# Last item divided on chip by products with constant selections, and the last block's output projection, layer norm and first MLP steps tile by tile

## The chip, the cores and the metric

The kernel runs on one core of a Trainium2 chip. The metric is the device time of one execution in microseconds (us); the median of three runs stands for a kernel. A profiled execution is a further run of its own, with its own time.

## The reference

One transformer layer on 2048 rows of 512 numbers, 32 heads of width 16, a hidden width of 1792, all float32:

```python
x = A_x
h = x + _A_ref(_layernorm(x, axis=-1), A_wqkv, A_wo)     # softmax attention, then @ wo
h2 = h + _B_ref(_layernorm(h, axis=-1), B_w1, B_w2)      # silu(z @ w1) @ w2
return h2
```

## The kernel before

**Precision.** A float32 product is made of three products of rounded operands (type float32r): high x high, low x high, high x low. `product` (L101) yields these three matmuls for each chunk of 128 contraction rows, 512 columns each. "Split" below means a copy to the rounded high part and a subtraction for the low part (`low`, L89).

**Attention.** The work goes in 32 items (`ITEMS`): an item is four heads for one block of 512 query rows, eight items to a block. In an item, 16 steps (`c`) each make four score products (`scores`, L463), four exponentials on ACT and, two steps later, four products with the values (`values`, L474), which accumulate in the one PSUM bank `pv`; row 16 of each head's 32 rows is the softmax denominator. `finish_item` (L489) copies `pv` to `pvs` and sends it on by DMA: denominators to DRAM and back as 16 per row (`sums`), a reciprocal on DVE (`invert`), to DRAM again and back broadcast over each head's 16 rows (`spread`, tile `den`), and, for each pair of items, one multiplication (`divide`) of a quarter of `ot`. `ot` holds attention's output of a block, transposed, in four chunks of 128 features for four tiles (`t`) of 128 rows; items 30 and 31 fill the lower and the upper 64 partitions of the last chunk.

**After a block**: output projection with `wo` (`project_rows`, L564), addition of the input rows and statistics (`add_rows`, L572), normalization (`normalize`, L158, on DVE), transposition on TensorE with a split into `hth` and `htl` (`turn`, L161), then the MLP (`mlp`, L581): 14 hidden chunks `f`, each with 12 matmuls for the first product, SiLU on ACT, a split, and 12 matmuls (three for each of the four tiles) for the second product, one chunk later. For the first three blocks this lies among the next block's attention. The last block has nothing beside it: `finish_last` (L649) runs it after the last value product.

**Order.** Every engine's instructions are pinned to the order in which the code issues them, and `soon(n, fn)` places a function n steps later. So an instruction that waits holds up all that stand behind it on its engine. Bank pools: `st` has four PSUM banks, `sm` three, `pv` one. Weight halves rotate through two buffers per name, raw weights through four.

Of the kernel before, what the change touches and what calls it, by code (L numbers as in the profile page):

```python
# [9 lines left out]
F32 = mybir.dt.float32  # L10
# [4 lines left out]
ALU = mybir.AluOpType  # L15
# [44 lines left out]
def attention_mlp_kernel(ctx: ExitStack, tc: tile.TileContext, x, wqkv, wo, w1, w2, out):  # L60
# [100 lines left out]
    def turn(src, dst_h, dst_l):  # L161

        ps = bank("ps_tr").rearrange("p (c n) -> p c n", n=P)
# [298 lines left out]

    def scores(g, k):  # L463
# [25 lines left out]
    def finish_item(i):  # L489
# [3 lines left out]
        act("copy", pvs, pv)  # L493
        dma(dn[i], pvs.rearrange("(k r) n -> k r n", r=32)[:, DH, :])
# [7 lines left out]
    rcs = {}  # L502
# [18 lines left out]
    def divide(i):  # L521

        o = ot[i // 8 % 2][:, :, i % 8 // 2, :]
        if i < ITEMS - 1:
            pool("tensor_tensor", o, o, den[i // 2], ALU.mult)
        else:
            dve("tensor_tensor", o, o, den[i // 2], ALU.mult)
# [15 lines left out]
    def split_weights(kind, f, engine):  # L543
        if f < FC:
            w = raw_w.pop((kind, f))
            wh, wl = ws[kind, f] = [gp.tile([P, 512], F32R, name=kind + part) for part in "hl"]
            act("copy", wh, w)
# [30 lines left out]
    def turn_rows(t):  # L578
        turn(hx.pop(t), hth[:, :, t * P:(t + 1) * P], htl[:, :, t * P:(t + 1) * P])

    def mlp(b, beside):  # L581
        engine = "pool" if beside else "dve"
# [3 lines left out]

        def second(f, gh, gl):
            w2h, w2l = ws.pop(("w2", f))
            if f == 0:
                acc.append(bank("ps_acc"))  # L590
            for t in range(4):
                weave(product(acc[t], lambda c: gh[:, t * P:(t + 1) * P], lambda c: gl[:, t * P:(t + 1) * P],
                              lambda c: w2h, lambda c: w2l, 1, start=f == 0, stop=f == FC - 1),
                      beside if f < FC - 1 else None)
                if f == FC - 1:
                    n = 4 * b + t
                    h = rows_of(b, t)
                    dve("tensor_tensor", h, acc[t], h, ALU.add)
                    dma(out[n * P:(n + 1) * P, :], h)

        last = None
        for f in range(FC):
            tick()
            if f < 2:
# [4 lines left out]
            split_weights("w1", f + 1, engine)  # L609
            split_weights("w2", f, engine)  # L610
# [3 lines left out]
            g, gh, gl = (bp.tile([P, 512], dt, tag="pt", name=name)  # L614
                         for name, dt in (("g", F32), ("gh", F32R), ("gl", F32R)))
            act("activation", g, ps, AF.Silu)
            act("copy", gh, g)
            low(gl, g, gh)
            if last:
                second(*last)  # L620
            last = (f, gh, gl)
        if b < NB - 1:

            act("activation", small.tile([P, 1], F32, name="sw"), ident[:, :1], AF.Exp)
        second(*last)
# [22 lines left out]

    def finish_last(pending):  # L649

        b, i = NB - 1, ITEMS - 1
        O = ot[b % 2]
# [12 lines left out]
        for t in range(4):  # L665
            run(project_rows(t, ps[t], range(3), stop=False))
        divide(i)
        for t in range(4):
            act("copy", os[t][0][:, 3:], O[:, t, 3:])
            low(os[t][1][:, 3:], O[:, t, 3:], os[t][0][:, 3:])  # L670
        act("activation", small.tile([P, 1], F32, name="sw"), ident[:, :1], AF.Silu)
        found = {}
        for t in range(4):
            run(project_rows(t, ps[t], [3], start=False))
            found[t] = add_rows(b, t, ps[t])
            if t > 0:
                normalize(hx[t - 1], rows_of(b, t - 1), *found[t - 1])
        normalize(hx[3], rows_of(b, 3), *found[3])
        for t in range(4):
            turn_rows(t)  # L680
        mlp(b, None)
# [19 lines left out]
    for g in range(groups):  # L701
# [20 lines left out]
        if g == groups - 4:  # L722
            for t in range(4):
                load_rows(NB - 1, t)
            for w in first_weights.values():
                load_weights(*w)
# [44 lines left out]
```

## Time and profile before

| | us |
|---|---|
| median of 3 runs (lowest, highest) | 1742.24 (1742.16, 1743.16) |
| profiled execution, its time | 1743.91 |
| span of that execution | 1742.1 |
| end of the last exponential | 1633.4 |
| last matmul begins | 1737.7 |

Times in the profile count from the start of the span. A row of a timeline has the start, the duration, engine, line and operation, then out<-in, shape and count; in brackets stand the idle time before it and what ended that. PE are matmuls, PEld the loads of the stationary operand, DVE, ACT and POOL the other engines, SP issues the DMAs. All matmuls of products have line 67, vector operations line 84, activations and copies line 81, POOL operations line 74, transpositions line 70: one helper records each kind, so groups are told apart by their tiles.

### The profile page before, as it was taken

The page shows a single profiled execution, that of the slowest core. Times are in us where ns is not written, and L with a number is a line of the kernel's source. Part 1 is how long each engine was busy: PE and PEld are TensorE (multiplying, and loading weights), DVE is VectorE, ACT ScalarE, POOL GpSimd, SP SyncE. Part 2 cuts the span into 40 slices and gives each one's busy share as a digit, 9 for nine tenths or more (in the row PEclk, how much of TensorE's full clock was granted, in tenths as well). Part 3 has the DMA queues.
Part 4 walks back from the last instruction along what each step waited for, and adds up shares of the span by engine and source line. Part 5 has one row for each costly group of instructions (what it writes and reads, how often), then busy time and mean ns, then how long its engine had stood idle before and what let it go on. Part 6 is the DMA issues. An engine that isn't in the chain of part 4 may idle for free.

```text
span 1742.1 us, 28292 instructions
## 1 busy us (share of the span) xinstructions
PE 1690.5 (97%) x10466; PEld 655.0 (38%) x10466; DVE 1461.3 (84%) x2392; ACT 1262.3 (72%) x2507; POOL 229.2 (13%) x312
## 2 busy tenths in 40 slices
PE   7999999999999999999999999999999999999899
PEld 5666322222245532222245532222245532221377
DVE  6899899999978889999978889999978889994243
ACT  4223699999953269999953269999963279999643
POOL 2123200000033300000033300000033300000000
PEclk9999999999999999999999999999999999999999
DMA  5334301111212111111213111111222111100232
GB/s 184 100 92 151 110 30 32 36 50 34 63 56 88 55 48 31 35 50 36 62 57 88 56 47 31 35 45 41 62 68 77 55 48 32 36 8 11 64 91 73
DMA packets 102211, 103.11 MB, mean 59 GB/s; under 512 B 20344, under 2 KB 78776, under 8 KB 102072
## 3 DMA queue, kind: packets, MB, share of 16 engines
q1 hardware_dynamic: 102072, 101.30, 19.9%
q8 instruction: 82, 1.34, 0.3%
q14 instruction: 57, 0.47, 0.1%
HBM read 77.86 MB, written 17.30 MB: 55 GB/s over the span
## 4 chain that ended last, share of the span: by engine, by line
PE 51%; ACT 36%; DVE 10%; issue 1%; DMA 1%; SPq 1%; POOL 0%; ACTq 0%; POOLq 0%; DVEq 0%
ACT pt L81 35%; PE pv L67 19%; PE ps_s L67 8%; PE ps_m L67 7%; DVE mx L206 6%; PE ps_qk L67 5%; PE ps_acc L67 5%; PE ps_v L67 3%; PE ps_wo L67 2%; DVE gl L84 2%; PE ps_tr L70 1%; DVE ot L84 1%; PE ps_w L67 1%; ACT pvs L81 1%; DMA w<-in_B_w_dram 0%
## 5 line engine op out<-in xcount | busy, mean ns | idle before, releaser
L206 DVE TENSOR_REDUCE mx<-ps_m 128x1 f32<-128x512 f32 x2048 | 1283.4, 684 | 124.3 <-PE ps_m L67 97.2
L81 ACT ACTIVATE pt<-ps_s 128x512 f32<-128x512 f32 x2048 | 1018.7, 645 | 33.8 <-PE ps_m L67 33.3
L67 PE MATMUL ps_s<-qs,ks 64*128 64x512 f16 x2048 | 550.8, 381 | 9.6 <-ACT pt L81 1.8
L67 PE MATMUL pv<-pt,va 128*17 128x512 f32 x4096 | 540.8, 601 | 1.0
L67 PE MATMUL ps_m<-ks,qs 48*128 48x512 f16 x2048 | 528.5, 382 | 8.9 <-DVE mx L206 7.1
L67 PEld LDWEIGHTS <-ks 64*128 64x128 f16 x2048 | 152.8, 95 | 538.3 <-issue 433.5
L67 PEld LDWEIGHTS pv<-pt,va 128*17 128x17 f32 x4096 | 68.8, 95 | 242.3 <-issue 226.1
L67 PEld LDWEIGHTS <-qs 48*128 48x128 f16 x2048 | 123.5, 94 | 84.2 <-issue 76.6
L81 ACT ACTIVATE g<-pv 128x512 f32<-128x512 f32 x52 | 31.1, 597 | 146.3 <-PE pv L67 146.3
L74 POOL TENSOR_SCALAR nm<-nm 128x16 f32<-128x16 f32 x32 | 8.3, 259 | 681.9 <-DVE nm L213 662.0
L84 DVE TENSOR_TENSOR gl<-g,gh 128x512 fp32r<-128x512 f32 x56 | 58.8, 1049 | 44.3 <-ACT gh L81 44.3
L67 PE MATMUL ps_acc<-w2h,gh 128*128 128x512 f32 x224 | 92.1, 411 | 0.0
L67 PE MATMUL ps_acc<-w2l,gh 128*128 128x512 f32 x224 | 91.5, 409 | 0.0
L81 ACT CAST w2h<-w 128x512 fp32r<-128x512 f32 x56 | 34.8, 621 | 73.7 <-POOL w1l L74 41.0
L67 PE MATMUL ps_acc<-w2h,gl 128*128 128x512 f32 x224 | 88.2, 394 | 0.0
L67 PE MATMUL pv<-hth,w1l 128*128 128x512 f32 x208 | 87.4, 420 | 0.0
L67 PE MATMUL pv<-htl,w1h 128*128 128x512 f32 x208 | 83.8, 403 | 0.0
L67 PE MATMUL pv<-hth,w1h 128*128 128x512 f32 x208 | 83.8, 403 | 0.0
L74 POOL TENSOR_TENSOR w1l<-w,w1h 128x512 fp32r<-128x512 f32 x42 | 54.2, 1291 | 153.4 <-ACT w1h L81 139.6
L74 POOL TENSOR_TENSOR w2l<-w,w2h 128x512 fp32r<-128x512 f32 x42 | 53.7, 1278 | 57.3 <-ACT w2h L81 57.3
L81 ACT ACTIVATE ks<-ps_qk,qk_s 128x512 f32<-128x512 f32 x24 | 16.5, 687 | 56.9 <-PE ps_qk L67 56.9
L74 POOL TENSOR_TENSOR ot<-ot,den 128x512 f32<-128x512 f32 x15 | 19.1, 1275 | 268.8 <-DMA den<-dr 255.4
(100 smaller groups left out, 1209.2 us busy)
## 6 DMA issues: line engine op xcount, KB each, us to landing
w<-in_B_w_dram SPq DMA_DIRECT2D x112, 256.0 KB
ks<-kd SPq DMA_DIRECT2D x120, 192.0 KB
qs<-qd SPq DMA_DIRECT2D x128, 48.0 KB
kd<-sh SPq DMA_DIRECT2D x16, 256.0 KB
qd<-sh SPq DMA_DIRECT2D x16, 256.0 KB
ot<-pvs SPq DMA_DIRECT2D x128, 32.0 KB
den<-dr SPq DMA_DIRECT2D x128, 32.0 KB
hx<-in_A_x_dram SPq DMA_DIRECT2D x16, 256.0 KB
```

The costliest lines, as they stand in the source:

```text
L67: tc.keep_in_program_order(nc.tensor.matmul(*a, **k))
L70: tc.keep_in_program_order(nc.tensor.transpose(*a))
L74: tc.keep_in_program_order(getattr(nc.gpsimd, op)(*a, **k))
L81: pin(getattr(nc.scalar, fn)(*a, **k))
L84: pin(getattr(nc.vector, fn)(*a, **k))
L206: pin(nc.vector.tensor_reduce(mx[i][:, j, a, qt, kb:kb + 1], ps, axis=AX.X, op=ALU.max))
```

## The change

1. **The last item (31)** isn't sent through DRAM. Two constant 128x128 selections, made on POOL before the attention loop, multiply `pvs` on TensorE in plain float32: `ps_d` gets each head's denominator on that head's 16 rows, `ps_o` the head's output. DVE takes the reciprocal of 64x512 and multiplies. Item 30 is divided by itself on 64 partitions.
2. **Splits of the last block** move into item 31, on DVE: the first three chunks of `ot`, item 30's half of the fourth, and the first two chunks of `w1` (high part too). They go into `hth` and `htl`, which are free then. The loads of rows and weights come some steps earlier.
3. **Tile by tile**: each tile is projected, added, normalized (tiles 0 to 2 on POOL, tile 3 on DVE) and transposed for itself, and `begin(t)` makes the first product of hidden chunks 0 and 1 for that tile alone: 24 matmuls of 128 columns.
4. **MLP of the last block**: written out as a loop, with the second product two chunks behind the first; the first products of chunk 2 onwards go to `sm` banks.

```diff
+    for k, (a, j) in enumerate(HEADS):
+        rows = slice(64 + 16 * (2 * a + j), 80 + 16 * (2 * a + j))
+        pool("tensor_copy", sel_o[:, rows], ident[:, 32 * k:32 * k + 16])
+        pool("tensor_copy", sel_d[:, rows], ident[:, 32 * k + DH:32 * k + DH + 1].to_broadcast([P, 16]))
...
     def finish_last(pending):
...
-        for t in range(4):
-            os[t] = [bp.tile([P, DC, P], F32R, tag="pt", name=name) for name in ("oh", "ol")]
-            act("copy", os[t][0][:, :3], O[:, t, :3])
-            low(os[t][1][:, :3], O[:, t, :3], os[t][0][:, :3])
         for g in pending:
             values(g)
-        agenda.clear()
-        sums(i)
-        invert(i)
-        spread(i)
-        split_weights("w1", 0, "dve")
-        ps = [bank("ps_wo") for _ in range(4)]
-        for t in range(4):
-            run(project_rows(t, ps[t], range(3), stop=False))
-        divide(i)
...
+        pvs = last.pop()
         act("activation", small.tile([P, 1], F32, name="sw"), ident[:, :1], AF.Silu)
+        ps_o, ps_d = bank("ps_o"), bank("ps_d")
+        ps_rows = [bank("ps_wo", "sm") for _ in range(3)] + [bank("ps_wo")]
+        first = [project_rows(t, ps_rows[t], range(3), stop=False) for t in range(4)]
+        for _ in range(3):
+            next(first[0])
+        mm(ps_d, sel_d, pvs, start=True, stop=True)
+        mm(ps_o, sel_o, pvs, start=True, stop=True)
+        o = bp.tile([P, 512], F32, tag="pt", name="o")
+        dve("reciprocal", o[64:], ps_d[64:])
+        dve("tensor_tensor", o[64:], ps_o[64:], o[64:], ALU.mult)
+        act("copy", hth[64:, DC - 1, :], o[64:])
+        low(htl[64:, DC - 1, :], o[64:], hth[64:, DC - 1, :])
...
+        run(first[0], first[1])
+        begun = [bank("ps_w1") for _ in range(2)]
+        def begin(t):
+            cols = slice(t * P, (t + 1) * P)
+            for f in range(2):
+                w1h, w1l = (w.rearrange("p (c n) -> p c n", n=P) for w in ws["w1", f])
+                run(product(begun[f][:, cols], lambda c: w1h[:, c, :], lambda c: w1l[:, c, :],
+                            lambda c: hth[:, c, cols], lambda c: htl[:, c, cols], DC))
...
+        rest(0)
+        rest(1)
+        run(first[2])
+        rest(2)
+        add(0)
+        norm(0)
+        add(1)
+        norm(1)
+        turn_first(0)
+        run(first[3])
+        rest(3)
+        add(2)
+        norm(2)
+        turn_first(1)
+        turn_second(0)
+        begin(0)
+        add(3)
+        norm(3)
+        turn_second(1)
+        turn_first(2)
+        begin(1)
+        turn_first(3)
+        turn_second(2)
+        begin(2)
+        turn_second(3)
+        begin(3)
...
-        if g == groups - 4:
-            for t in range(4):
-                load_rows(NB - 1, t)
-            for w in first_weights.values():
-                load_weights(*w)
+        if i == ITEMS - 1:
+            if c < 4:
+                load_rows(NB - 1, c)
+                split_early(c)
+            if c == 4:
+                for f in range(3):
+                    load_weights("w1", f)
+                for f in range(2):
+                    soon(5, split_weights, "w1", f, "dve", "dve")
```

`rest(t)` is the fourth chunk's three matmuls of the projection, `add` and `norm` are the addition with statistics and the normalization, `turn_first` the four transpositions and the high copy on ACT, `turn_second` the low part on DVE.

DVE, from the last maximum's reduction (`nm<-mx`, the row ahead of these) through the projection, before:

```order
L84 RECIPROCAL rc<-rc 128x16
L84 TENSOR_TENSOR ol<-ot_2033,oh 128x384 x4
L84 RECIPROCAL rc<-rc 128x16
L84 TENSOR_TENSOR w1l<-w,w1h 128x512
L84 TENSOR_TENSOR ot_2033<-ot_2033,den 128x4x128
L84 TENSOR_TENSOR ol<-ot_2033,oh 128x128 x4
L84 TENSOR_TENSOR ot_2033<-ps_wo,hx 128x512
L84 BN_STATS st<-ot_2033 128x6
L84 BN_AGGR mv<-st 128x2
```

and in the change, from item 30's reciprocal on:

```order
L84 RECIPROCAL rc<-rc 128x16
L84 CAST w1h<-w 128x512
L84 TENSOR_TENSOR w1l<-w,w1h 128x512
L84 CAST w1h<-w 128x512
L84 TENSOR_TENSOR w1l<-w,w1h 128x512
L84 CAST hth<-ot_2033 64x512
L84 TENSOR_TENSOR htl<-ot_2033,hth 64x512
L84 RECIPROCAL o<-ps_d 64x512
L84 TENSOR_TENSOR o<-ps_o,o 64x512
L84 TENSOR_TENSOR htl<-o,hth 64x512
L84 TENSOR_TENSOR ot_2033<-ps_wo,hx 128x512
L84 BN_STATS st<-ot_2033 128x6
```

The reciprocal of 128x16 behind a DMA has become one of 64x512 behind a matmul, and the splits now stand ahead of it.

ACT, from the last copy of `pv` to the weights of the MLP's first chunks, before:

```order
L81 COPY pvs<-pv 128x512
L81 CAST w1h<-w 128x512
L81 CAST oh<-ot_2033 128x128 x4
L81 ACT_TABLE_LOAD
L81 ACTIVATE sw<-ident 128x1
L81 CAST hth<-ps_tr 128x4x128 x4
L81 CAST w1h<-w 128x512
L81 CAST w2h<-w 128x512
L81 ACTIVATE g<-ps_w_21406 128x512
L81 CAST gh<-g 128x512
```

and in the change:

```order
L81 COPY pvs<-pv 128x512
L81 ACT_TABLE_LOAD
L81 ACTIVATE sw<-ident 128x1
L81 CAST hth<-o 64x512
L81 CAST hth<-ps_tr 128x4x128 x4
L81 ACTIVATE g<-ps_w_21310 128x512
L81 CAST gh<-g 128x512
L81 CAST w1h<-w 128x512
L81 ACTIVATE g<-ps_w_21311 128x512
L81 CAST gh<-g 128x512
```

The next high part of `w1` (chunk 2) now stands behind the SiLU and its copy, where before chunk 1's stood ahead of them.

More of the change, by code (lines that the diff above doesn't have):

```diff
@@ L613, in mlp, with gate, second @@
                           lambda c: hth[:, c, :], lambda c: htl[:, c, :], DC), beside)
[L614 to L618, printed above, removed]
-            if last:
[L620 to L625, printed above, removed]
+            gs = gate(ps)
+            if last:
+                second(b, *last, acc, beside)
+            last = (f, *gs)
+        act("activation", small.tile([P, 1], F32, name="sw"), ident[:, :1], AF.Exp)
+        second(b, *last, acc, beside)
+    def gate(ps):
+        g, gh, gl = (bp.tile([P, 512], dt, tag="pt", name=name)
+                     for name, dt in (("g", F32), ("gh", F32R), ("gl", F32R)))
+        act("activation", g, ps, AF.Silu)
+        act("copy", gh, g)
+        low(gl, g, gh)
+        return gh, gl
+    def second(b, f, gh, gl, acc, beside):
+        w2h, w2l = ws.pop(("w2", f))
+        while f == 0 and len(acc) < 4:
+            acc.append(bank("ps_acc"))
+        for t in range(4):
+            weave(product(acc[t], lambda c: gh[:, t * P:(t + 1) * P], lambda c: gl[:, t * P:(t + 1) * P],
+                          lambda c: w2h, lambda c: w2l, 1, start=f == 0, stop=f == FC - 1),
+                  beside if f < FC - 1 else None)
+            if f == FC - 1:
+                n = 4 * b + t
+                h = rows_of(b, t)
+                dve("tensor_tensor", h, acc[t], h, ALU.add)
+                dma(out[n * P:(n + 1) * P, :], h)
     found = {}
@@ new lines, in add, with norm, turn_first @@
+        def add(t):
+            h = rows_of(b, t)
+            dve("tensor_tensor", h, ps_rows[t], hx[t], ALU.add)
+            found[t] = statistics(h)
+        def norm(t):
+            if t < 3:
+                mv, rs = found[t]
+                pool("tensor_scalar", hx[t], rows_of(b, t), mv[:, 0:1], rs, op0=ALU.subtract, op1=ALU.mult)
+            else:
+                normalize(hx[t], rows_of(b, t), *found[t])
+        parts = {}
+        def turn_first(t):
+            ps = bank("ps_tr", "sm").rearrange("p (c n) -> p c n", n=P)
+            for c in range(4):
+                tr(ps[:, c, :], hx[t][:, c * P:(c + 1) * P], ident)
+            h = hth[:, :, t * P:(t + 1) * P]
+            act("copy", h, ps)
+            parts[t] = ps, h
```

103 lines of the change are left out of this document (62 added, 41 removed).

## The prediction, as put on record before the run

> **What bounds the kernel now.** The page first: engine shares and the slices of the span.
>
> ```profile
> PE 1690.5 (97%) x10466; PEld 655.0 (38%) x10466; DVE 1461.3 (84%) x2392; ACT 1262.3 (72%) x2507; POOL 229.2 (13%) x312
> PE   7999999999999999999999999999999999999899
> ```
>
> PE is busy for 97%; of the 40 slices only the first and the third last are below nine tenths. TensorE's order in the two kernels is the same up to the last value product, but for names of buffers, so the question is the stretch behind it. Next the table of stretches, cut where PE's work changes (columns: stretch, length, then busy time and count of PE, PEld, DVE, ACT, POOL, clock, DMA):
>
> ```profile
> 1605.90:1634.50 28.60, 27.45 (x181) 5.04 (x181) 0.95 (x3) 28.60 (x61) 0.00 (x0) 1.00 0.27 75
> 1634.50:1643.00 8.50, 8.50 (x40) 6.65 (x36) 2.06 (x5) 1.48 (x4) 0.00 (x0) 1.00 0.10 18
> 1643.00:1646.70 3.70, 0.15 (x2) 0.01 (x1) 0.72 (x2) 0.36 (x2) 0.00 (x0) 1.00 0.55 157
> 1646.70:1651.40 4.70, 4.60 (x12) 3.04 (x12) 4.34 (x12) 2.03 (x5) 1.16 (x3) 0.64 0.04 16
> 1651.40:1658.50 7.10, 3.57 (x17) 2.30 (x17) 6.18 (x13) 2.42 (x5) 2.58 (x6) 0.74 0.01 2
> 1658.50:1663.00 4.50, 4.50 (x13) 3.54 (x14) 1.84 (x3) 0.96 (x2) 0.00 (x0) 0.65 0.35 117
> 1663.00:1736.10 73.10, 73.10 (x316) 59.17 (x315) 25.81 (x39) 31.36 (x53) 0.00 (x0) 1.00 0.26 76
> ```
>
> Item 31 is ACT's (28.60 of 28.60), with DVE and POOL free. Then come 36 matmuls of the projection (8.5 us), a hole of 3.7, the projection's last 12 at a clock of 0.64, a chain of normalizations and transpositions with PE half idle, a first MLP product at 0.65, and from 1663.0 to the end PE without a gap. The chain of waits says what fills hole and chain:
>
> ```profile
> 1638.73 1.75 DMA rc<-dn
> 1640.78 1.40 DMA dr<-rc
> 1643.48 1.81 DMA den<-dr
> 1645.61 0.70 DVE ot L84
> ...
> 1656.08 0.56 DVE hx L84
> ...
> 1658.47 4.49 PE ps_w L67 x12
> 1662.96 2.80 PE pv L67 x12
> 1665.76 2.76 PE ps_acc L67 x12
> 1668.52 2.81 PE pv L67 x12
> ```
>
> The DMA round trip ends in the division at 1645.61; DVE's chain holds the first product back to 1658.47. A product at full clock takes 2.81 (0.234 a matmul), a second one 2.76. Everything behind is PE's, and has the same matmuls in both kernels. So I compare one point: where chunk 0's second product begins with products 0, 1 and 2 done. Before, products 0 to 2 and chunk 0's second product are done at 1668.52 + 2.81 = 1671.33, so the point stands at 1671.33 - 2.76 = 1668.57.
>
> **The division.** ACT's four splits no longer stand ahead of the copy of `pv`; the last value product sets its start:
>
> ```profile
> 1631.77 2.77 PE L67 MATMUL pv<-pt,va 128*17 128x512 f32 x24
> L67 PE MATMUL pv<-pt,va x4096: 592/593/1061, 201.0 to 1633.9; 128*17 128x512 f32 x196
> L81 ACT COPY pvs<-pv 128x512 f32<-128x512 f32 x32 | 20.1, 629 | 2.1 <-PE ps_n L70 1.6 <-PE pv L67 0.5
> L84 DVE RECIPROCAL qk_e<-qk_s x1: 164/164/164, 26.7 to 26.7; 128x1 f32<-128x1 f32 x1
> L84 DVE RECIPROCAL rc<-rc 128x16 f32<-128x16 f32 x32 | 7.8, 244 | 25.9 <-DMA rc<-dn 25.9
> L84 DVE TENSOR_TENSOR ot<-ot,den 128x512 f32<-128x512 f32 x1 | 0.7, 691 | 4.3 <-DMA den<-dr 4.3
> ```
>
> The values end at 1631.77 + 2.77 = 1634.54, the copy (0.63) at 1635.2. The 24 records are six sets of four side by side, two for each float32 product, so a set takes (2.77 - 0.59)/5 = 0.435 and a plain float32 product of 512 columns 0.87. `ps_d` starts at 1635.25 and lands at 1636.3 (0.435 + 0.593). The reciprocal's price is unseen at 512 columns. From 1 to 16 columns it grew by 244 - 164 = 80 ns, 5.33 ns a column; so 0.16 + 511 x 0.00533 = 2.9. Its bounds are 0.69, the multiplication at one pass, and 7.8 (244 ns for every 16). I take 2.9: same operation, two sizes. It ends at 1639.2, the multiplication at 1639.9, ACT's copy (0.62) at 1640.55, the low part (0.69) at 1641.25.
>
> PE meanwhile does the two selections and 15 projection matmuls: 1635.25 + 1.74 + 15 x 0.234 = 1640.5. The fourth chunk's second matmul needs the low part: a stall of 0.6 to 0.8. So the 3.7 us hole shrinks to that, paid with 1.74 of new PE work.
>
> The Trainium skill, "VectorE: DVE Perf Modes", section "First, the fixed hardware budget", says that the reciprocal divides iteratively with a repeat count of 8. If that meant eight cycles at its 0.96 GHz, the estimate were 512 x 8 / 0.96 = 4.3 us and the sum 1.4 later; the two rows give 5.1 such cycles a column, and I go by them.
>
> **The chain of tiles.** Rows for its steps, tile 1's normalization then POOL's nearest:
>
> ```profile
> 1650.03 0.69 DVE L84 BATCH_NORM_STATS2 st<-ot 128x6 f32<-128x512 f32 x1
> 1651.03 0.42 POOL L74 TENSOR_SCALAR rs<-mv 128x1 f32<-128x1 f32 x1 [0.64 <-DVE mv L84]
> 1651.54 0.56 POOL L74 TENSOR_TENSOR rs<-rs,expo 128x1 f32<-128x1 f32 x1
> L74 POOL TENSOR_TENSOR ot<-ot,den 128x512 f32<-128x512 f32 x15 | 19.1, 1275 | 268.8 <-DMA den<-dr 255.4 <-DMA ks<-kd 13.3
> 1651.43 0.66 PE L70 MATMUL ps_tr<-ident,hx 128*128 128x128 f32 x4
> L70 PE MATMUL ps_tr<-ident,hx x64: 272/273/476, 496.6 to 1657.4; 128*128 128x128 f32 x64
> ```
>
> From 1641.3 two matmuls of `rest(0)`, `rest(1)`, nine of `first[2]` and `rest(2)` keep PE for 17 x 0.234, to 1645.25. DVE's addition and statistics are 0.69 + 0.69 + some 0.2 for the aggregate = 1.6, from the landing of `rest(0)` at 1641.9 to 1643.55; POOL's root adds 1.05. POOL's normalization of 128x512 is unseen: bounds 0.56 (DVE's own, in the chain above) and 1.28 (POOL's two-input form); I take 1.2, near POOL's row. So tile 0 is ready at 1645.85: a stall of 0.6. The next tiles come from POOL every 2.2 and are ready before PE asks. Four transpositions are 0.45 of PE's time, the twelve matmuls of `first[3]` and `rest(3)` 2.8, four more transpositions 0.45: `begin(0)` starts at 1649.6.
>
> **The narrow matmuls** decide: 96 of 128 columns in place of 24 of 512 (24 x 0.234 = 5.6 us). No row has a float32r matmul below 512 columns. Nearest:
>
> ```profile
> 1634.47 0.19 PEld L67 LDWEIGHTS ps_wo<-wo_h,oh 128*128 128x128 f32 x1 [0.85 <-ACT oh L81]
> 1634.47 0.51 PE L67 MATMUL ps_wo<-wo_h,oh 128*128 128x512 f32 x1
> 1634.58 0.19 PEld L67 LDWEIGHTS ps_wo<-wo_h,ol 128*128 128x128 f32 x1
> 1635.05 0.40 PE L67 MATMUL ps_wo<-wo_l,oh 128*128 128x512 f32 x1
> ```
>
> The first load is followed 0.11 later by the second, and its matmul is 0.11 longer (0.51 against 0.40): a load occupies the array for 0.11, however wide the matmul. Four 128-column transpositions in 0.66 with 0.273 for one give 0.11 to 0.13 each as well. So the price per matmul lies between 0.06 (a quarter of 0.234) and 0.234 (no gain from narrowness); I take 0.115, load-bound.
>
> Then 96 x 0.115 + two sets of transpositions (0.9) end `begin(3)` at 1661.6. The DVE and ACT parts are ready in time: tile 3's addition (from 1649.3), root and normalization end at 1652.6 and tile 1's low part, queued behind them on DVE, at 1653.3, when `begin(1)` has just started. Behind `begin(3)` comes a new wait. Chunk 2's weights need the buffers of chunk 0, read until 12 matmuls before the end (1660.2, landing 1660.4), and stand behind SiLU and copy. How long that series takes, the steady MLP shows:
>
> ```profile
> 1715.96 0.60 ACT L81 ACTIVATE g<-pv 128x512 f32<-128x512 f32 x1 [2.42 <-PE pv L67]
> 1717.12 0.62 ACT L81 CAST w1h<-w 128x512 fp32r<-128x512 f32 x1
> 1717.86 0.68 DVE L84 TENSOR_TENSOR w1l<-w,w1h 128x512 fp32r<-128x512 f32 x1
> ```
>
> That is 2.58 us: the low part of `w1` is there at 1663.0, a stall of about 1.2 in PE. Eleven matmuls of chunk 2 are left (2.57): the point is reached at **1665.57, 3.0 us earlier** than before's 1668.57. Later chunks have the old rhythm, with the second product two chunks behind, so their splits have more room, not less. With the price x of a narrow matmul the point moves by 84x - 12.65 us (96 in the path, 12 taken off since the weights' wait starts 12 earlier): zero at x = 0.15.
>
> The page "TensorE: Matmul & The Clock Gate" of the Trainium skill, section "Back-to-back issue gap", has 81 ns for sustained 128-column pairs. Worked out as an estimate that would put the sum at -5.8; no run here shows it for float32r, and the load of 0.11 speaks against it.
>
> **At nothing** I cost: item 31's new splits (12 DVE operations of at most 0.7; DVE is busy 0.95 of 28.6; were it not free, each would cost that), the earlier loads on SP, the SiLU table (under the selections; ACT waits until 1639.9), the banks (each one taken anew has its reader done by then), and POOL's ten small operations before the loop, where it idles 20.15 us:
>
> ```profile
> 214.37 1.28 POOL L74 TENSOR_TENSOR wo_l<-w,wo_h 128x512 fp32r<-128x512 f32 x1 [20.15 <-PE ps_s L67]
> ```
>
> Sum: 1743.91 - 3.0 = 1740.9 for a run like the profiled one, which lies 1.7 above the median; the same 3.0 off 1742.24 gives **1739.2**. That is -0.17%, and about 0.2% (3.5 us) is what a measurement of this kernel can tell from no change.
>
> **The rivals.** *R1, slower: narrow float32r at the plain float32 rate.* 0.87 per 512 columns is 0.217 per 128. Place: the four `begin`s; price 84 x 0.217 - 12.65 = +5.6, so 1747.9; it decides from 0.15 on. For it: the operands are float32 in the rows. Against: at 512 columns float32r takes a quarter of float32's time. Chance 0.15.
>
> *R2: load and matmul don't overlap* at this width: 0.11 + 0.053 = 0.16, or PEld's whole 0.188. +0.8 to +3.1, so 1743.0 to 1745.3. Against: transpositions overlap. Chance 0.13.
>
> *R3: the clock.* Two rows of stretches:
>
> ```profile
> 1644.40:1647.80 3.40, 1.11 (x4) 0.86 (x5) 1.60 (x6) 1.44 (x5) 0.00 (x0) 1.00 0.52 164
> 1647.80:1651.30 3.50, 3.50 (x9) 2.19 (x7) 3.36 (x8) 0.94 (x2) 1.06 (x3) 0.52 0.00 0
> ```
>
> 3.4 us with PE a third busy are followed by as long at half clock. Load-bound narrow matmuls keep the array half used, and the stall of 1.2 stands right behind them; one such stretch costs 1.7, leaving -1.3, 1740.9. A reciprocal of 4.3 would end near there too. Chance 0.10.
>
> **How the numbers follow.** Forecast 0.57: x from 0.107 to 0.13 and POOL's bounds give -4.6 to -1.5, 1737.6 to 1740.7. R1 0.15, R2 0.13, R3 0.10, and 0.05 for a stall I don't see, counted as slower. The range, 1737.4 to 1745.6, holds the forecast, R3 and R2, 0.80. Faster by over 0.2% (under 1738.8) is nearly half of the forecast, 0.27; slower (over 1745.7) R1 and the 0.05, 0.20; within, 0.53.
>
> **What will show it.** Right: no DMA between the last value product and the projection's end; a 64x512 reciprocal of 2.9; narrow matmuls 0.11 to 0.12 apart; an ACT wait ahead of chunk 2's product; the clock at 1.00 throughout. Wrong: narrow starts over 0.15 apart, a reciprocal over 4, POOL's normalization over 1.5, or a clock of 0.5 within the `begin`s.

## The result and the profile after

The changed kernel takes **1741.08 us** (median of 20 runs, 1736.14 to 1748.58), the kernel before 1741.31 (20 runs beside them, 1736.69 to 1744.06); the ratio is 1.0005, 95% interval [0.9993, 1.0016]. No difference can be told. The forecast gain of 3.0 us would be a ratio of 0.9983, which lies outside this interval: the time came out within the range, which contains the old time as well, but the gain did not come.

The profiled execution took 1741.04 us with a span of 1739.3, against 1743.91 and 1742.1 before. But most of these 2.8 us lie ahead of the change. The last block's first projection matmul starts at 1634.47 before and at 1632.15 after, 2.3 us earlier, and the attention ahead of it is the same work. At the last exponential of item 24, at 1294.6 us before, the traces are 0.8 us apart, at that of item 25 they are 2.3 apart. One stretch between the two shows why; its row in the table of stretches of the kernel before (columns: stretch, length, busy time and count of PE, PEld, DVE, ACT, POOL, clock, DMA):

```profile
1412.30:1415.70 3.40, 3.39 (x15) 0.59 (x15) 1.56 (x4) 2.43 (x6) 0.67 (x3) 0.52 0.02 5
```

and the same stretch in the changed kernel:

```profile
1412.30:1415.70 3.40, 3.37 (x28) 0.94 (x23) 2.65 (x5) 3.40 (x10) 0.42 (x2) 1.00 0.00 0
```

Before, TensorE ran at half clock there and did 15 matmuls in place of 28; that comes and goes between executions (7 of the 14 traces have half clock there). So spans of two executions can't be compared for an edit at the end. I compare **the tail**: from the first projection matmul to the end of the span.

| | before | after | forecast |
|---|---|---|---|
| tail, us | 107.6 | 107.15 | 104.6 |
| first projection matmul to chunk 0's second product, with products 0 to 2 done | 34.10 | 33.85 | 31.1 |
| granted clock up to that point | 0.5 and 1.0 by turns | 1.00 | 1.00 |

The tail is 0.5 us shorter, not 3.0, though its clock stayed at 1.00. The page's share of PE is what it was:

```profile
PE 1692.2 (97%) x10542; PEld 659.6 (38%) x10542; DVE 1465.4 (84%) x2394; ACT 1257.8 (72%) x2498; POOL 237.4 (14%) x326
```

The chain that ended last, changed kernel (start, length, engine and tile):

```profile
1634.09 3.37 DVE o L84
...
1638.93 0.70 DVE htl L84
...
1639.68 0.74 PE ps_wo L67 x2
...
1643.15 2.08 POOL hx L74
...
1646.18 2.08 POOL hx L74
...
1649.22 2.08 POOL hx L74
...
1652.19 0.55 DVE hx L84
1652.74 0.61 DVE htl L84
...
1653.39 2.68 PE ps_w L67 x22
...
1662.42 0.70 DVE w1l L84
...
1663.16 2.83 PE ps_w L67 x11
1666.00 2.76 PE ps_acc L67 x12
```

There is no DMA in it any more: the round trip is gone. In its place stand the reciprocal (3.37) and then POOL, three times 2.08 at a distance of 3.04. What PE waited for between 1632 and 1667 (engine, tile, what it waited for: us, times, longest):

```profile
PE ps_tr L70 <- POOL hx L74: 1.4, 1, 1.4
PE ps_w L67 <- DVE htl L84: 1.0, 1, 1.0
PE ps_wo L67 <- ACT hth L81: 0.6, 1, 0.6
PE ps_w L67 <- ACT w1h L81: 0.5, 1, 0.5
PE ps_w L67 <- DVE w1l L84: 0.3, 1, 0.3
PE ps_wo L67 <- DVE htl L84: 0.2, 1, 0.2
```

That is 4.0 us of waits. The wait of 1.0 for DVE's `htl` goes back to POOL too, by way of DVE's order. Two rows of DVE show it:

```profile
1652.19 0.55 DVE L84 TENSOR_SCALAR hx<-ot,mv,rs 128x512 f32<-128x512 f32 x1 [1.80 <-POOL rs L74]
1652.65 1.28 DVE L84 TENSOR_TENSOR htl<-ps_tr,hth 128x512 fp32r<-128x512 f32 x2
```

Tile 3's normalization on DVE sat 1.80 us for its root, which stood behind tile 2's normalization on POOL, and tile 1's low part, which PE wanted, is issued behind that normalization on DVE, though DVE was free.

The narrow matmuls, the first and the twenty-first of one row of them:

```profile
1659.32 0.27 PE L67 MATMUL ps_w<-hth,w1h 128*128 128x128 f32 x1
1661.56 0.27 PE L67 MATMUL ps_w<-htl,w1h 128*128 128x128 f32 x1
```

Twenty distances in 2.24 us: 0.112 each. So 96 of them are 10.75 us where 24 of full width, 0.234 each, are 5.62: **5.1 us more of PE's time**, set against the waits that they fill.

### The profile page after: what moved, and what is told of

It is laid out like the page before. It is cut to its first block, busy times and chain, and to the rows that moved or that the text cites. A ratio compares the mean times of both kernels' runs of the same rounds, so it can differ in the third digit from the quotient of the medians.

```text
span 1739.3 us, 28446 instructions
## 1 busy us (share of the span) xinstructions
PE 1692.2 (97%) x10542; PEld 659.6 (38%) x10542; DVE 1465.4 (84%) x2394; ACT 1257.8 (72%) x2498; POOL 237.4 (14%) x326
## 4 chain that ended last, share of the span: by engine, by line
PE 51%; ACT 37%; DVE 10%; issue 1%; POOL 1%; DMA 1%; SPq 0%; ACTq 0%; POOLq 0%; DVEq 0%
ACT pt L81 35%; PE pv L67 17%; PE ps_s L67 8%; PE ps_m L67 7%; DVE mx L206 6%; PE ps_acc L67 5%; PE ps_qk L67 5%; PE ps_w L67 3%; PE ps_v L67 3%; PE ps_wo L67 2%; DVE gl L84 2%; PE ps_tr L70 1%; ACT pvs L81 1%; DVE ot L84 1%; POOL hx L74 0%
## 5 line engine op out<-in xcount | busy, mean ns | idle before, releaser
L81 ACT ACTIVATE g<-pv 128x512 f32<-128x512 f32 x39 | 23.3, 597 | 118.9 <-PE pv L67 118.9
L67 PE MATMUL pv<-hth,w1l 128*128 128x512 f32 x156 | 66.6, 427 | 0.0
L67 PE MATMUL pv<-hth,w1h 128*128 128x512 f32 x156 | 63.1, 405 | 0.0
L67 PE MATMUL pv<-htl,w1h 128*128 128x512 f32 x156 | 62.9, 403 | 0.0
L74 POOL TENSOR_TENSOR ot<-ot,den 128x512 f32<-128x512 f32 (+1 forms) x16 | 20.3, 1271 | 291.6 <-DMA den<-dr 278.8
```

What stands on the lines that cost most here:

```text
L67: tc.keep_in_program_order(nc.tensor.matmul(*a, **k))
L74: tc.keep_in_program_order(getattr(nc.gpsimd, op)(*a, **k))
L81: pin(getattr(nc.scalar, fn)(*a, **k))
```

## The experiments

All ratios are to the kernel before in runs on the same chip. "Tail" is as above, from the profiled execution.

### Normalizations on DVE instead of POOL

```diff
-            if t < 3:
-                mv, rs = found[t]
-                pool("tensor_scalar", hx[t], rows_of(b, t), mv[:, 0:1], rs, op0=ALU.subtract, op1=ALU.mult)
-            else:
-                normalize(hx[t], rows_of(b, t), *found[t])
+            normalize(hx[t], rows_of(b, t), *found[t])
...
         add(1)
-        norm(1)
+        norm(0)
```

(Tile 1's normalization then stands behind tile 2's addition, tile 2's behind tile 0's low part, and tile 3's behind tile 1's low part, which so goes ahead of it.)

> All four normalizations on DVE, each one behind the next tile's addition; POOL keeps only the roots. Tail below means the time from the first projection matmul of the last block to the end of the span: 107.6 us before, 107.15 after. Theory POOL (POOL's normalization, 2.08 us a tile where I had put 1.2, sets the chain of tiles and makes PE wait 1.45 ahead of tile 0's transpositions and 0.97 in tile 1's first narrow products): those waits fall to 0.5 and 0, the tail to 104.9, the median to about 1738.8. Rival (the clock or the narrow matmuls are what ate the gain): tail within 0.5 of 107.15.

Measured: 1737.86 us (6 runs), ratio 0.9971 [0.9959, 0.9983]; tail 106.25, with one stretch of 3.4 us at half clock, from 1658.6 to 1662.0, behind the narrow products. That can cost up to 1.7, so the tail is 104.6 to 106.25 without it. PE's waits for POOL are gone; for the normalized tiles this is left:

```profile
PE ps_tr L70 <- DVE hx L84: 0.3, 1, 0.3
```

What follows: the slow normalization on POOL, with the order behind it, was on the path, worth 0.9 us in the traces as they are and up to 2.6 at equal clock. With both gone the kernel is faster than before.

The edit changes two things, and the order alone, with the normalizations left on POOL, was not run. In the changed kernel tile 1's high part is there at 1649.78, DVE is idle from 1650.39 to 1652.19, and PE begins to wait for the low part (0.69) at 1652.42. By an estimate from these rows the order alone would have taken away the wait of 1.0. The wait of 1.4 ahead of tile 0's transpositions ends with POOL's normalization in either order.

### No narrow products

```diff
         def begin(t):
-            cols = slice(t * P, (t + 1) * P)
+            if t < 3:
+                return
+            cols = slice(0, 4 * P)
```

> The first products of hidden chunks 0 and 1 are made after the last transposition, with 24 matmuls of 512 columns in place of 96 of 128. Theory (a narrow float32r matmul is bound by its 0.11 us load): the begins' 10.6 us of PE work become 5.6, which start only when tile 3 is turned (some 22 us into the tail), so the tail is 104.2 at full clock; but PE then has little to do for 5 us, and every stretch of 3.4 us at half clock that follows costs up to 1.7, so 104 to 107.5. Rival (filling the chain's gaps with narrow work is worth what it costs): tail over 107.5.

Measured: 1740.31 us (11 runs), ratio 0.9988 [0.9979, 0.9996]; tail 105.8, within the 104 to 107.5 expected, with 3.4 us at half clock (1653.2 to 1656.7). PE now waits for POOL more:

```profile
PE ps_tr L70 <- POOL hx L74: 3.7, 2, 2.2
```

Even so the tail is 1.3 us shorter than with narrow products. What follows: with POOL's pace as it is, "tile by tile" for both chunks costs more than it hides.

### The changed kernel with its holes filled

Extra products into the free bank `pv`, used by nobody, stand where PE waited (2, 6, 4 and 3 of them):

```diff
+        def fill(n):
+            for _ in range(n):
+                mm(pv, wo_h[:, 0, :P], wo_h[:, 0, :], start=True, stop=True)
...
+        fill(2)
...
         norm(1)
+        fill(6)
...
         turn_first(2)
+        fill(4)
...
         begin(3)
+        fill(3)
```

> The changed kernel with 15 extra matmuls whose result nobody reads, placed in PE's four waits of the tail (2, 6, 4 and 3 of 0.23 us), so that PE isn't idle there. Theory clock (the runs of the change near 1747 are those in which the clock fell in the tail): in the profile the tail stays at 107.2 plus or minus 0.4, and the timed runs lose their upper end: none over 1744.5, median 1739.5 to 1741. Rival (the spread comes from elsewhere): a quarter of the runs over 1744.5, as without them.

Measured: 1742.21 us (12 runs, 1735.3 to 1743.71), ratio 0.999 [0.9981, 0.9999]; tail 107.1 at clock 1.00. The median missed what was expected by about 1 us. The upper end is what the clock theory asked for: with filled holes no run was above 1744.5 or under a mean clock of 0.992; the changed kernel had five of twenty above, with mean clocks of 0.988 to 0.991. But there are no runs of the changed kernel without the fillers beside these, so it isn't shown that the fillers made the difference.

### A late first tile

Four POOL multiplications, results unused, ahead of tile 0's normalization:

```diff
                 mv, rs = found[t]
+                for _ in range(4 if t == 0 else 0):
+                    pool("tensor_tensor", o, rows_of(b, 0), rows_of(b, 0), ALU.mult)
```

> Four extra POOL multiplications of 1.28 us (their result isn't used) stand ahead of tile 0's normalization, so PE waits some 6.5 us ahead of the first transpositions. Theory (narrow matmuls use the array half of the time and do not bring a fallen clock back): the clock stays at 0.5 through all four begins, narrow matmuls stand 0.21 apart, the begins take some 20 us and the tail is 107.15 + 5.1 + 10 = 122. Rival (any steady work brings the clock back within some 3.4 to 6.8 us): the clock is 1.0 again by tile 1's begin, tail 113 to 115.

Measured: one run, 1747.09 us; tail 113.2. Stretches of this kernel:

```profile
1644.90:1648.30 3.40, 0.00 (x0) 0.00 (x0) 0.55 (x2) 0.00 (x0) 3.24 (x4) 1.00 0.00 0
1648.30:1651.70 3.40, 2.19 (x8) 1.90 (x9) 0.42 (x1) 0.59 (x1) 3.21 (x4) 0.52 0.00 0
1651.70:1655.10 3.40, 3.40 (x9) 2.63 (x8) 0.27 (x1) 0.00 (x0) 3.21 (x4) 0.50 0.02 5
1655.10:1658.50 3.40, 3.40 (x31) 3.29 (x29) 1.82 (x4) 0.59 (x1) 1.23 (x3) 0.98 0.00 0
```

A stretch without PE work is followed by half clock, and after one stretch full of work the clock is back. My expectation that it stays low through the narrow products failed here: the full-width matmuls of `first[3]` and `rest(3)` came first, and brought it back. That left the question whether narrow products alone can.

### The changed kernel once more

> The changed kernel once more, unaltered, on one chip with the experiments beside it. Theory (its tail is 0.5 us shorter than before's when the clock holds, and the rest of a run's time is decided by how often the clock falls): ratio to before 0.998 to 1.001, tail in the profile 107.0 to 108.9, and the times of single runs follow the mean clock of the run, 1.4 us for each 0.001. Rival (the spread is not the clock): no such line.

Measured: 1747.77 us (11 runs), ratio 1.0019 [1.0010, 1.0028]. The profiled execution took 1743.69, its tail **112.25**. Its waits are those of the table above (1.5, 1.0, 0.6, 0.2). What differs is the clock:

```profile
1649.50:1652.90 3.40, 2.40 (x23) 2.25 (x20) 1.74 (x3) 0.58 (x1) 0.17 (x1) 1.00 0.00 0
1652.90:1656.40 3.50, 3.50 (x20) 3.50 (x19) 0.69 (x1) 0.59 (x1) 0.00 (x0) 0.53 0.00 0
1656.40:1659.80 3.40, 3.40 (x17) 3.40 (x18) 0.00 (x0) 0.00 (x0) 0.00 (x0) 0.50 0.00 0
1659.80:1663.20 3.40, 3.40 (x18) 3.40 (x18) 0.00 (x0) 0.77 (x2) 0.00 (x0) 0.50 0.00 0
1663.20:1666.60 3.40, 3.40 (x14) 3.03 (x14) 1.66 (x3) 2.57 (x5) 0.00 (x0) 0.50 0.18 11
1666.60:1670.00 3.40, 3.40 (x16) 2.78 (x15) 1.56 (x4) 1.92 (x5) 0.00 (x0) 0.98 0.48 156
```

The first stretch holds the wait of 1.0 for `htl`, with narrow products around it. Then the clock is at half for four stretches, though PE's rows fill each of them, and it comes back only behind the stretch in which chunk 2's full-width product began. Narrow products stand 0.21 us apart meanwhile:

```profile
1656.40 0.41 PE L67 MATMUL ps_w<-hth,w1h 128*128 128x128 f32 x1
1656.61 0.41 PE L67 MATMUL ps_w<-hth,w1l 128*128 128x128 f32 x1
```

What was expected (a tail of 107.0 to 108.9, a ratio of 0.998 to 1.001) fell. What follows: the same program, with the same waits, has a tail of 107.15 or of 112.25, by whether the clock falls among the narrow products. Two of the eleven runs were at 1741.72 and 1743.69 with mean clocks of 0.993 and 0.991; nine were at 1746.8 to 1749.05 with 0.989 or 0.988. Only the profiled one has a trace. A mean clock doesn't say where the clock fell: that the nine lost it at this place too fits their clocks, and is not shown.

### The kernel before with its holes filled

The same fillers in the kernel before's tail, 13 in the hole ahead of the fourth chunk, 12 ahead of the transpositions and 2 ahead of the first MLP product:

```diff
+        fill(13)
         divide(i)
...
         for t in range(4):
+            fill((0, 5, 5, 2)[t])
             turn_rows(t)
+        fill(2)
         mlp(b, None)
```

> The kernel before with 27 extra matmuls whose result nobody reads, 13 of them in the hole that the division's DMAs leave, 5, 5 and 2 ahead of tiles 1 to 3's transpositions and 2 ahead of the first MLP product, so that PE isn't idle there. Theory (the clock that falls behind the hole costs before's tail 1.8 in the projection, some 0.9 in transpositions and 1.7 in the first product): clock 1.00 through the tail, tail 107.6 - 3 to 4 = 104, and a ratio to before of 0.997 to 0.9985, which would make the filled kernel faster than the change. Rival (the chain on DVE sets the tail, whatever the clock): tail 106.5 to 108.

Measured: 1742.12 us (11 runs), ratio 0.9987 [0.9978, 0.9996]; tail 106.6 at clock 1.00. The theory's tail of 104 fell, the rival's 106.5 to 108 held: half clock costs the kernel before about 1.1 us of its 107.6, and the rest of the tail is the chain of the division and of DVE. So at a clock of 1.00 in both, the changed kernel's 107.15 is no gain at all: the 0.5 us in the table above is less than what half clock took from the kernel before.

The clocks fit as well: on this chip the eleven runs with fillers have mean clocks of 0.992 to 0.995, the 22 of the kernel before 0.988 to 0.991.

### The changed kernel without the reciprocal

```diff
-        dve("reciprocal", o[64:], ps_d[64:])
+        dve("tensor_copy", o[64:], ps_d[64:])
```

> The changed kernel with a plain copy of 64x512 in place of the reciprocal, so the last item's half chunk is multiplied by the denominators, not divided. Theory (the reciprocal's 3.36 us is on the path, in series with the chain of tiles): the copy takes 0.6 to 0.7, PE's waits for the fourth chunk (0.84) vanish, tile 0's addition starts 1.2 us earlier and everything behind it: tail 107.15 - 1.2 = 105.95. Rival (POOL's cadence hides it): tail unchanged within 0.3.

Measured: one run, 1747.49 us; tail 112.5, with half clock from 1653.7 to 1670.8, five stretches, so neither of the expected tails can be judged by it. Up to there the reciprocal's share can be read: the first addition stands 6.92 us behind the first projection matmul, 8.29 in the changed kernel, and the wait in `begin(1)` ends at 19.88, against 21.24. Both waits of the fourth chunk are gone:

```profile
PE ps_tr L70 <- POOL hx L74: 1.5, 1, 1.5
PE ps_w L67 <- DVE htl L84: 1.0, 1, 1.0
```

So the path is 1.4 us shorter up to the narrow products, and then the clock took 5. The reciprocal is on the path; its full 2.7 us above the copy (3.36 against 0.69) are not, since PE's projection products fill part of that time.

### The division on chip alone

The kernel before with part 1 only: the selections' products stand behind tile 0's first nine projection matmuls, the rest of the tail is the old one.

```diff
-        sums(i)
-        invert(i)
-        spread(i)
...
+            if t == 0:
+                mm(ps_d, sel_d, pvs, start=True, stop=True)
+                mm(ps_o, sel_o, pvs, start=True, stop=True)
+        o = bp.tile([P, 512], F32, tag="pt", name="o")
+        dve("reciprocal", o[64:], ps_d[64:])
+        dve("tensor_tensor", O[64:, :, 3, :], ps_o[64:].rearrange("p (t n) -> p t n", n=P),
+            o[64:].rearrange("p (t n) -> p t n", n=P), ALU.mult)
```

> The kernel before with the first part of the change alone: the last item divided on chip, the rest of the tail in the old order. By my theory that part removes the wait for the transfers (the fourth chunk's projection starts about 2 us earlier than before and the tensor engine has no long wait there), so the tail from the first projection matmul to the span's end is about 104.4 us where the kernel before took 107.6 and, with fillers in its holes, 106.6; ratio about 0.998. Rival: the division is hidden behind the other three chunks' products anyway and VectorE's chain of additions and normalizations sets the end: tail 106.5 or more, ratio 0.9990 to 1.0005.

Measured: 1739.77 us (11 runs), ratio 0.9986 [0.9977, 0.9995]; tail 105.5, between the theory's 104.4 and the rival's 106.5. Stretches:

```profile
1640.70:1644.10 3.40, 3.40 (x16) 2.76 (x15) 0.98 (x3) 1.30 (x2) 0.00 (x0) 1.00 0.00 0
1644.10:1647.50 3.40, 1.80 (x10) 1.01 (x8) 3.26 (x8) 0.00 (x0) 1.74 (x4) 1.00 0.00 0
1647.50:1650.90 3.40, 0.76 (x6) 0.51 (x6) 3.15 (x7) 1.17 (x2) 1.43 (x4) 1.00 0.02 5
1650.90:1654.30 3.40, 2.39 (x9) 1.59 (x10) 2.76 (x5) 1.63 (x4) 0.56 (x1) 0.52 0.00 0
```

The projection runs through without a hole, and DVE's chain of four tiles (busy 3.15 to 3.26 of 3.40) leaves PE idle behind it, with half clock as before. So part 1 is worth **2.1 us** here, less than the hole of 3.7 that it closes. Parts 2 to 4 together then cost 1.6 (105.5 to 107.15), and more at equal clock, since this tail has 6.8 us at half clock and the changed kernel's has none.

### One chunk narrow, normalizations on DVE

Both lessons together: the normalizations and the order of the first experiment, and only chunk 0 taken tile by tile; chunk 1 is one full-width product behind the last tile.

```diff
-            for f in range(2):
+            for f in range(1):
...
-            if f < 2:
+            if f < 1:
                 ps = begun[f]
             else:
-                ps = bank("ps_w", "sm")
+                ps = begun[1] if f == 1 else bank("ps_w", "sm")
```

> As the experiment with all normalizations on DVE, and only hidden chunk 0 is begun tile by tile; chunk 1's product is made with 512 columns after it. Theory (48 narrow matmuls fill the gaps of the chain, the other 48 only cost 2.6 us more than the wide ones, and with chunk 1 behind chunk 0 the wait for chunk 2's weights is covered): tail 107.15 - 2.3 - 3.6 = 101.3 at full clock, up to 103 with one stretch at half clock, ratio to before 0.995. Rival (a fallen clock takes it back): tail over 104.

Measured: 1738.03 us (6 runs), ratio 0.9964 [0.9952, 0.9976]; tail **101.4** at clock 1.00, as expected. Against the first experiment, with two chunks narrow, that is 4.8 us (up to 1.7 of it the clock): 48 narrow products are 5.4 us, 12 full-width ones 2.8, and chunk 2's waits for its weights (0.8) go as well.

### The division in two halves side by side

The kernel of the last experiment, with the selections' products taken 256 columns at a time onto partitions 0 to 63 and 64 to 127:

```diff
-        mm(ps_d, sel_d, pvs, start=True, stop=True)
-        mm(ps_o, sel_o, pvs, start=True, stop=True)
+        for ps, sel in ((ps_d, sel_d), (ps_o, sel_o)):
+            for rows, cols in halves:
+                mm(ps[rows, :256], sel[:, 64:], pvs[:, cols], start=True, stop=True)
...
-        dve("reciprocal", o[64:], ps_d[64:])
-        dve("tensor_tensor", o[64:], ps_o[64:], o[64:], ALU.mult)
+        dve("reciprocal", inv[:, :256], ps_d[:, :256])
+        for rows, cols in halves:
+            dve("tensor_tensor", o[64:, cols], ps_o[rows, :256], inv[rows, :256], ALU.mult)
```

> The kernel of e8 with the last item's division in two halves side by side: the selections' products are taken 256 columns at a time onto partitions 0 to 63 and 64 to 127, so that one reciprocal of 128x256 stands for that of 64x512, and two multiplications of 64x256 follow. If a reciprocal is paid by the column, as 3.36 us for 512 columns in the changed kernel's trace says, it takes about 1.7 us here; the first addition then comes about 1.3 us earlier behind the first projection matmul, the projection no longer waits for the fourth chunk (0.8 us), and from the first projection matmul to the span's end there are about 100.1 us (e8: 101.4); ratio to the kernel before about 0.9955 (e8: 0.9964). Rival: the reciprocal is off the path once the normalizations are on VectorE, since the additions and row statistics of four tiles queue there anyway: the same stretch stays within 0.3 us of 101.4 and the ratio within 0.0005 of 0.9964.

Measured: **1734.32 us** (5 runs), ratio 0.9949 [0.9936, 0.9963]; tail 99.4 at clock 1.00. The row of the reciprocal:

```profile
1633.96 1.76 DVE L84 RECIPROCAL inv<-ps_d 128x256 f32<-128x256 f32 x1 [14.09 <-PE ps_d L67]
```

and all that is left of PE's waits from 1630 to 1680:

```profile
PE ps_tr L70 <- DVE hx L84: 0.3, 1, 0.3
```

Half the columns take 1.76 where 512 took 3.36, and the tail is 2.0 us shorter, 0.7 more than I had reckoned. This version beats the kernel before by 0.5% and the changed one with it.

### A late first low part

The changed kernel with nine DVE multiplications, results unused, ahead of tile 0's low part, so that PE stands idle right ahead of the narrow products:

```diff
+            for _ in range(9):
+                dve("tensor_tensor", o, rows_of(b, 0), rows_of(b, 0), ALU.mult)
             low(htl[:, :, t * P:(t + 1) * P], ps, h)
```

> The changed kernel with nine more multiplications on VectorE (about 0.69 us each, results unused) ahead of the low part of the first normalized tile, so that the tensor engine stands idle for 4 to 5 us right ahead of the 128-column products. My theory, that these products, which use the array for about half of the time, cannot bring a fallen clock back: the clock stands at 0.5 from there until the whole-width products of the third chunk, pairs of the narrow matmuls are about 0.21 us apart where they were 0.11, and the tail from the first projection matmul to the span's end is about 121 us (the changed kernel: 107.2 at full clock, 112.3 in e5, where the clock fell by itself). Rival: any steady stream brings it back: 1.0 again within 6.8 us of the first narrow product, tail 115 or less.

Measured: one run, 1757.95 us; tail **121.3**, the theory's 121. Half clock from 1654.9 to 1682.2, eight stretches; three of them and the one behind:

```profile
1658.30:1661.70 3.40, 3.40 (x19) 3.40 (x18) 1.15 (x2) 0.00 (x0) 0.37 (x1) 0.50 0.00 0
...
1668.60:1672.00 3.40, 3.40 (x18) 3.40 (x18) 0.68 (x1) 0.00 (x0) 0.00 (x0) 0.50 0.00 0
...
1678.80:1682.20 3.40, 3.40 (x9) 2.64 (x8) 1.89 (x3) 1.59 (x3) 0.00 (x0) 0.50 0.27 94
1682.20:1685.60 3.40, 3.40 (x16) 2.78 (x15) 1.35 (x3) 2.26 (x4) 0.00 (x0) 0.98 0.45 142
```

The stretches with 18 or 19 matmuls of 128 columns each (narrow products, in some with four transpositions), without a gap in PE's rows, don't bring the clock back; the one with 9 full-width products does. The rival, that any steady stream does (115 or less), is out.

### One chunk narrow, normalizations on POOL

The edit of "one chunk narrow" alone, in the changed kernel.

> The changed kernel with its normalizations on GpSimd as they are, but only the first chunk of w1 taken tile by tile; the second is one whole-width product of 2.8 us behind the last tile. The question is whether the doubled price of the narrow products (two chunks: 2.8 us more than whole-width) adds to the slow normalizations or lies beside them. My theory, that it partly lies beside them (GpSimd delivers a tile each 3.0 us, two chunks take 2.8 us per tile, one chunk 1.4): from the changed kernel's rows the first chunk's last tile would end 1658.2 on its time scale, the second chunk 1661.0, where now the narrow products end at 1662.1, so the tail from the first projection matmul to the span's end is 106.0 at full clock (the changed kernel: 107.2), with the tensor engine waiting for GpSimd's tiles for 2 us or more. Rival: the two prices add up, the tail falls by the whole 2.8 us to 104.4, as it does with the normalizations on VectorE. Ratio 0.998 to 1.000 by the theory, 0.9975 or less by the rival.

Measured: 1745.46 us (12 runs), ratio 1.0006 [0.9996, 1.0017]; tail 110.9, with half clock from 1654.6 to 1668.2, four stretches. That decides nothing between the two figures, both made for full clock. What can be read is PE's waits for POOL, 2 us or more as the theory had it, and one behind them:

```profile
PE ps_tr L70 <- POOL hx L74: 2.4, 2, 1.5
PE ps_w L67 <- DVE htl L84: 1.2, 1, 1.2
```

With the waits left in, the clock fell here too; the same edit without POOL's waits (tail 101.4) kept it. How the two prices add up at full clock stays open.

## Why the prediction was right about the time and wrong about the gain

That the time fell into the range says nothing for the sum: the range, 1737.4 to 1745.6, contains the old time of 1742.24 as well. The sum itself missed by 2.5 of its 3.0 us in the tail, and without the half clock that the kernel before had there, by all of it. (The lower end of -4.6 does not come out of its terms either: 84 x 0.107 - 12.65 is -3.7, and a faster normalization can only take off the stall of 0.6, so -4.3. R2's 0.053 is in no row; a quarter of 0.234 is 0.059.)

**The division** was right in kind: no DMA is left between the values and the projection's end. The reciprocal took 3.36 where I took 2.9 from two small sizes, within the bounds; (3.36 - 0.164) / 511 is 6.25 ns a column. On the Trainium skill's repeat count of 8 ("VectorE: DVE Perf Modes", "First, the fixed hardware budget") my estimate was 4.3 us: that is too high by 0.9, and the measurement decides. The fourth chunk's second matmul came 0.7 us later than forecast on the same scale (1639.68 against 1641.3 - 2.3). What I had not seen is how little closing the hole is worth alone: 2.1 us of 3.7.

**The step that failed** is POOL's normalization, put at 1.2 between bounds of 0.56 and 1.28. It takes 2.08, outside the bounds, and over the 1.5 that the prediction had named as a sign of being wrong. The nearest row was an operation with two tensors and none of per-partition scalars, and I let it be the upper end. This mis-sized term counts twice. PE waits 1.45 for the first tile, 0.9 more than the 0.6 forecast; and "the next tiles come from POOL every 2.2 and are ready before PE asks" becomes 3.04 (2.08 and its two root operations), so that tile 3's root, DVE behind it and tile 1's low part behind that are late, and `begin(1)`, for which I had forecast no wait, waits 1.0. This second part needs DVE's order as well, in which the sum had no room: the low part was forecast at 1653.3, when `begin(1)` had just started. With the 0.7 of the division and 0.15 for all the rest, these make the 2.75 us by which the point was missed (1666.00 against 1665.57 - 2.32 = 1663.25). The first experiment shows that these waits hang on POOL and the order: with both changed they are 0.3 and nothing, and the tail is 104.6 to 106.25. That its lower end is the 104.6 forecast is chance, since DVE takes 0.55 and not the 1.2 of the sum.

**The narrow matmuls** were right: 0.112, forecast 0.115. R1 and R2 fall (0.15 to 0.217 needed), and so does the estimate of -5.8 from the 81 ns that the Trainium skill's page "TensorE: Matmul & The Clock Gate", section "Back-to-back issue gap", gives for pairs of 128 columns. **The ring of `w1`** was right too: 0.8 of waits, 1.2 forecast. So is the 5.1 us that narrowness costs in the sum; I had it in the term, but did not ask whether one chunk would fill the waits as well. It does, once the tiles come on time: that is 2.6 of the 4.8 us between the first and the one-chunk experiment, and the ring's waits are 0.8 more.

**The costs at nothing** held where they can be read: the last exponentials of items 30 and 31 are 31.85 us apart in both traces, so item 31's new splits cost nothing.

**R3, the clock,** was right in kind and wrong in its size. The place that I gave it, the stall behind the narrow products, is where the clock fell in the first experiment, for one stretch. In the repeated run of the changed kernel it fell earlier, at the wait in `begin(1)` that I had not forecast. I priced one stretch at half clock at 1.7 and thought the clock would then return. It costs 1.3 a stretch there (5.1 over four), but narrow products don't bring it back, so it lasts until chunk 2: four stretches in the changed kernel, five and eight in variants of it, and a tail of 112 to 121. The same program has tails of both kinds, and its ratio is 1.0005 in one series and 1.0019 in another; that the clock in the tail makes this difference is likely, but shown for the profiled runs alone. What the Trainium skill's page "TensorE: Matmul & The Clock Gate" says in "What's actually happening", that the clock falls after a whole idle window of about 3.4 us and returns after one busy one, agrees here in the length (27.3 us in eight stretches) and not in the rest: it fell behind a stretch in which PE's rows fill 2.40 of 3.40 us, and in the last-but-one experiment five full ones with 128-column products and transpositions alone did not bring it back.

**The comparison itself.** The 2.8 us between the two profiled spans look like my 3.0, by accident: 2.3 of them lie ahead of the change.

## What to carry to other kernels

Cut a matmul into narrow pieces only as far as it fills waits that are there, and put the normalization that feeds it on the engine whose price for that very operation is in the trace; a row of another form is no upper bound. Read a change at the end of a kernel from a point in its own stage, not from the span. Where PE does narrow products, a wait among them can be dear: in four traces here the clock fell at such a wait and stayed down for four to eight stretches, until full-width work came.

## What the runs showed of the hardware

- A stream of 128-column float32r products with a few transpositions, without a gap in PE's rows, kept the clock at 1.00 where it was there (1654.3 to 1661.2 in the changed kernel's profile):

```profile
1650.90:1654.30 3.40, 2.43 (x22) 2.29 (x22) 1.74 (x3) 0.59 (x1) 1.17 (x3) 1.00 0.00 0
1654.30:1657.70 3.40, 3.40 (x33) 3.40 (x32) 0.52 (x1) 0.59 (x1) 0.00 (x0) 1.00 0.00 0
1657.70:1661.20 3.50, 3.50 (x34) 3.50 (x33) 0.17 (x1) 0.64 (x2) 0.00 (x0) 1.00 0.00 0
```

but did not restore it (the repeated run and the late first low part). The first of these rows, 2.43 of 3.40 busy, kept the clock; 2.40 in the repeated run lost it. No limit on PE's busy share lies between them: in the first experiment the clock fell behind a stretch with more, mostly of narrow products,

```profile
1655.20:1658.60 3.40, 2.57 (x19) 2.12 (x19) 1.29 (x2) 2.78 (x6) 0.00 (x0) 1.00 0.00 0
```

and in the repeated run it held behind one with 1.95 of 3.42 (1639.42 to 1642.84), mostly of full-width matmuls. What decides stays open.
- Over the 20 runs of the changed kernel the time follows the mean clock: 1736.14 at 0.997, 1748.58 at 0.988, so 1.4 us for each 0.001. One stretch of 3.4 us at half clock is about that much of the mean: 3.4 x 0.5 of 1740 us.
- POOL's normalization of 128x512 with two per-partition scalars takes 2.08 us, DVE's 0.55.
- A DVE reciprocal was paid by the column and not by the partition: 3.36 us for 64x512, 1.76 for 128x256.
